# Gateloop attention with mixture of depths: 128-token tiles in place of 32-token chunks

## The chip, the cores and the metric

One core of a Trainium2 chip. The metric is device time in microseconds, the median of three runs. The engines in the traces: PE is TensorE (PEld its weight loads), DVE VectorE, ACT ScalarE, POOL GpSimd, SP SyncE, which issues the loads and stores.

## The reference

Four batches, 8 heads, 768 tokens, head size 48. Each head keeps a complex 48 x 48 state that decays and turns by a gate of each token and takes in k v; the output is q times the real part. The heads side by side give 384 columns, on which a mixture of depths works: of each batch's 768 tokens the 128 with the largest score pass a two-layer network and are added back, times a sigmoid of their score.

```python
mag = np.sqrt(a_re * a_re + a_im * a_im)
scale = np.minimum(mag, 0.999) / (mag + 1e-06)
a_re_n, a_im_n = (a_re * scale, a_im * scale)
for t in range(S):
    ar, ai = (a_re_n[:, :, t, :, None], a_im_n[:, :, t, :, None])
    new_re = ar * S_re - ai * S_im
    new_im = ar * S_im + ai * S_re
    kv = np.einsum('bhd,bhe->bhde', k[:, :, t], v[:, :, t])
    S_re, S_im = (new_re + kv, new_im)
    y[:, :, t] = np.einsum('bhd,bhde->bhe', q[:, :, t], S_re)
...
for b in range(B):
    top_idx = np.argpartition(-scores[b], capacity)[:capacity]
    xe = x[b, top_idx]
    ye = np.maximum(xe @ w1, 0.0) @ w2
    g = 1.0 / (1.0 + np.exp(-scores[b, top_idx]))
    out[b, top_idx] = x[b, top_idx] + g[:, None] * ye
```

The inputs: a_re is uniform between 0.85 and 0.95, a_im normal with a spread of 0.1.

## The kernel before

The recurrence is turned into matmuls. The logs of the decays and the phases are summed along the tokens by triangular matrices on PE; their exponentials (E for the queries, Ei for the keys) and cosines and sines multiply q and k, so that a token pair's decayed score is a product of 96 numbers per head (48 cosine and 48 sine parts). A tile is 128 tokens; there are 24 tiles, six in a batch, and everything is float32.

- `gates(g)`, for a group of two tiles: logs and angles on ScalarE, GpSimd and DVE; `within` sums the log decays inside chunks of 32 tokens, relative to the chunk's middle (csl, L273); `across` gets the steps from middle to middle as 16 small matmuls (ms, L283) and a few DVE operations on m (L287 to L293); `phase` sums the turns of a tile (cst, L312) and adds the last row of the tile in front (L315), after which DVE takes the whole turns off (r and fg, L317 and L318); `absolute` and `sines` make cos and sin on ScalarE, for both tiles at once.
- `attention(g, c)`, for one tile: DVE turns q and GpSimd turns k (tq and tk, L352 and L355). `scores(hg)`, for four heads at a time: four PE transposes of q (L366) which ScalarE copies to SBUF (qT, L368), four of k (L371) which DVE copies in two halves of each chunk (kT, L376), then the scores of the first halves' keys against all queries (L383, 64 keys by 128 queries, PSUM partitions 0 to 63) and of the second halves' keys against the second halves' queries (L385, 64 by 64, PSUM partitions 64 to 127), and two predicated copies on DVE for the causal mask (L391). `inside` multiplies the masked scores with the values (L399), which for this are loaded a second time in another order (vh). Then for each of the four chunks `chunk(ci)`: DVE carries the state to the chunk's middle (G, L413), eight matmuls add its part to y (L415, 32 output rows), eight more form the chunk's own k v (d, L422, 32 tokens deep, 96 columns by 48), and DVE adds d to G (L428). `finish` copies y out and takes the score.
- `depths(b)`, for a batch: rank by comparing all scores, select 128 tokens, gather them (gx), two layers (hid, fin), scatter-add at the end.

The emitted order is woven: the gates run a group ahead of the scores, a tile's chunks run beside the next tile's scores, the depths a batch behind. A scheduler then sets each engine's queue, and the engines take their queues in order. PSUM has two buffers for csl, ms and cst together, two for the transposes (tp), and one each for the scores, d, y and the depths.

Of the kernel before, what the change touches and what calls it, by code (L numbers as in the profile page):

```python
# [14 lines left out]
OP = mybir.AluOpType  # L15
PSUM = bass.MemoryType.PSUM
# [5 lines left out]
CH = 32  # L22
HALF = CH // 2
NCH = P // CH
# Largest -log of a step's decay, exp(HALF * LNMAX) times a score still being a float32. A step that
# decays more counts as exp(-LNMAX).
LNMAX = 4.8
# [21 lines left out]
def kernel(  # L49
# [18 lines left out]
    DD = 2 * D  # L68
# [4 lines left out]
    C = 2  # L73
    W = C * DM
    GPB = NT // C
    NG = B * GPB
    NB = (capacity + P - 1) // P
    HG = 4

    singles = ctx.enter_context(tc.tile_pool(name="singles", bufs=1))  # L80
    ld = ctx.enter_context(tc.tile_pool(name="ld", bufs=2))
    tmp = ctx.enter_context(tc.tile_pool(name="tmp", bufs=1))
    grp = ctx.enter_context(tc.tile_pool(name="grp", bufs=2))
    pe_ = ctx.enter_context(tc.tile_pool(name="pe_", bufs=2))
    qkp = ctx.enter_context(tc.tile_pool(name="qkp", bufs=2))
    stp = ctx.enter_context(tc.tile_pool(name="stp", bufs=2))
    xp = ctx.enter_context(tc.tile_pool(name="xp", bufs=2))
    mod = ctx.enter_context(tc.tile_pool(name="mod", bufs=1))
    fp = ctx.enter_context(tc.tile_pool(name="fp", bufs=B if NB == 1 else 2))
    dr = ctx.enter_context(tc.tile_pool(name="dr", bufs=2, space=DRAM))  # L90
# [10 lines left out]
    def act(**kw):  # L101
        """An activation that needs its table: these stay in the order in which they are emitted."""
# [5 lines left out]
    def table(name):  # L108
        ins = nc.scalar.preload_act_table_set(name)
# [5 lines left out]

    def load(nm, src, g):
        b, s = divmod(g, GPB)
        t = ld.tile([P, C, DM], FP, tag=nm, name=nm, bufs=3 if nm == "v" else 2)
        nc.sync.dma_start(out=t, in_=src[b, s * C * P:(s + 1) * C * P].rearrange("(c p) m -> p c m", p=P))
        T[nm, g] = t.rearrange("p c m -> p (c m)")  # L120

    def load_halves(g):
        # the values again, the first halves of the chunks in front of the second ones
        b, s = divmod(g, GPB)
        t = ld.tile([P, C, DM], FP, tag="vh", name="vh", bufs=3)
        for c in range(C):
            t0 = (s * C + c) * P
            rows = v[b, t0:t0 + P].rearrange("(n f i) m -> f n i m", f=2, i=HALF)
            for f in range(2):
                nc.sync.dma_start(out=t[f * P // 2:(f + 1) * P // 2, c],  # L130
                                  in_=rows[f])
        T["vh", g] = t.rearrange("p c m -> p (c m)")

    def load_a(g):
        if g < NG:
            load("ar", a_re, g)
            load("ai", a_im, g)

    def load_qkv(g):
        if g < NG:  # L140
            for nm, src in (("q", q), ("k", k), ("v", v)):
                load(nm, src, g)
            load_halves(g)

    load_a(0)
    load_qkv(0)
    load_a(1)

# [10 lines left out]
    def keep(t, pattern, base, mul):  # L159
        nc.gpsimd.affine_select(out=t, in_=t, compare_op=OP.is_ge, fill=0.0, base=base, pattern=pattern,  # L160
                                channel_multiplier=mul)

    # causal[s, t]: s and t in one chunk, s <= t
    causal = ones([P, NCH, CH], "causal")
    keep(causal, [[-CH, NCH], [0, CH]], 0, 1)
    keep(causal, [[CH, NCH], [1, CH]], 0, -1)
    # wmat[s, t]: the steps between the chunk's middle and t, with their sign
    wmat = ones([P, NCH, CH], "wmat")
    keep(wmat, [[-CH, NCH], [0, CH]], 0, 1)
    keep(wmat, [[CH, NCH], [0, CH]], HALF - 1, -1)  # L170
    nc.vector.tensor_tensor(out=wmat, in0=causal, in1=wmat, op=OP.subtract)
    wmat = wmat.rearrange("p a b -> p (a b)")
    # between[s, c]: the steps from the middle of chunk c - 1 to that of chunk c; of the first chunk
    # those in this tile, and in the last column those from the last middle to the end
    between = ones([P, NCH + 1], "between")
    keep(between, [[-CH, NCH + 1]], HALF, 1)
    keep(between, [[CH, NCH + 1]], HALF - 1, -1)
# [5 lines left out]
    keep(last, [[0, P]], -(P - 1), 1)  # L183
    # earlier[i, j]: j < i
# [443 lines left out]
```

## Time and profile before

| what | value |
|---|---|
| runs | 878.3, 883.08, 887.25 us |
| median | 883.08 us |
| span of the profiled execution | 883.5 us |
| PE busy in it | 805.7 us |
| DVE busy in it | 410.5 us |
| ACT and POOL busy in it | 206.3 and 165.0 us |
| mean granted clock of TensorE | 0.629 |

The profiled execution has no time of its own beside its span; the span runs from the first to the last instruction and agrees with the median within 0.4 us. Busy times of engines overlap, so they don't add up. [...]

### The profile page before, as it was taken

To read this page: it belongs to the slowest core of one execution; us is meant where nothing else is said; L and a number is where in the kernel's file an instruction comes from. 1 tells how busy PE (TensorE), PEld (TensorE's weight loads), DVE (VectorE), ACT (ScalarE), POOL (GpSimd) and SP (SyncE) were. 2 spreads that over 40 slices of the span, in tenths; PEclk is the share of its full clock that TensorE was granted. 3 is DMA by queue.
4 is the path that set the end of the run, shared out by engine and by line. 5 is a ranking of instruction groups with operands and counts; after the bars stand their busy time and mean duration, and the time that the engine had idled before them with its cause. 6 is when DMAs were issued, how large, how long until landed. Compare 5 with 4: busy or idle time off the path is not lost. (4 is left out here: it accounts for less than half of the span.)

```text
span 883.5 us, 12759 instructions
## 1 busy us (share of the span) xinstructions
PE 805.7 (91%) x5452; PEld 669.5 (76%) x5452; DVE 410.5 (46%) x886; ACT 206.3 (23%) x296; POOL 165.0 (19%) x117
## 2 busy tenths in 40 slices
PE   1499999999999899999999989999999979999926
PEld 0388887887787688787887878889779759888824
DVE  5444734544426765424335654632533674543250
ACT  4241420321313213112221420511321311200000
POOL 6140500511302302111300400410220220100020
PEclk9975555555556587655557556855655756795559
DMA  8511201201203102011201301110210000000030
GB/s 234 185 55 46 81 1 54 72 2 58 69 1 92 52 19 64 19 27 46 72 10 45 99 1 36 56 35 1 67 60 1 28 10 1 10 10 1 10 54 10
DMA packets 25881, 39.57 MB, mean 45 GB/s; under 512 B 1736, under 2 KB 24928, under 8 KB 25824
## 3 DMA queue, kind: packets, MB, share of 16 engines
q1 hardware_dynamic: 25248, 37.96, 14.0%
q0 software_dynamic: 576, 0.79, 0.8%
q8 instruction: 43, 0.70, 0.4%
q14 instruction: 14, 0.11, 0.0%
HBM read 33.23 MB, written 5.52 MB: 44 GB/s over the span
## 5 line engine op out<-in xcount | busy, mean ns | idle before, releaser
L422 PEld LDWEIGHTS d<-v,tk 32*96 32x96 f32 x1472 | 217.7, 242 | 44.5 <-issue 14.6
L422 PE MATMUL d<-v,tk 32*96 32x48 f32 x1472 | 239.9, 330 | 11.1 <-POOL tk L355 6.2
L355 POOL TENSOR_TENSOR tk<-cos,ek 128x768 f32<-128x768 f32 x24 | 51.6, 2149 | 553.4 <-ACT cos L103 304.3
L415 PEld LDWEIGHTS y<-G,qT 96*32 96x32 f32 x1472 | 106.2, 153 | 27.7 <-issue 12.0
L415 PE MATMUL y<-G,qT 96*32 96x48 f32 x1472 | 121.9, 263 | 1.9 <-DVE G L413 1.9
L383 PE MATMUL at<-qT,kT 96*64 96x128 f32 x384 | 94.2, 396 | 0.0
L399 PEld LDWEIGHTS y<-vh,att 128*128 128x128 f32 x384 | 71.5, 272 | 11.8 <-issue 6.2
L368 ACT COPY qT<-tq 96x512 f32<-96x512 f32 x48 | 27.9, 582 | 219.5 <-PE tq L366 219.1
L399 PE MATMUL y<-vh,att 128*128 128x48 f32 x384 | 74.3, 351 | 2.4 <-DVE att L391 1.6
L391 DVE COPY_PREDICATED att<-ordered,at 128x256 f32<-128x256 uint32 x96 | 37.8, 426 | 79.6 <-PE at L385 79.3
L383 PEld LDWEIGHTS at<-qT,kT 96*64 96x64 f32 x384 | 62.0, 198 | 11.8 <-issue 3.6
L273 PE MATMUL csl<-ln,wmat 128*128 128x384 f32 x48 | 36.2, 884 | 30.1 <-DVE ln L265 30.1
L283 PEld LDWEIGHTS ms<-between,ln 128*96 128x96 f32 x384 | 56.5, 254 | 3.6 <-issue 3.3
L283 PE MATMUL ms<-between,ln 128*96 128x5 f32 x384 | 57.0, 285 | 0.9 <-issue 0.9
L371 PE MATMUL tk<-ident,tk 128*96 128x128 f32 x192 | 52.7, 399 | 1.3 <-ACT qT L368 1.3
L366 PE MATMUL tq<-ident,tq 128*96 128x128 f32 x192 | 53.9, 407 | 0.0
L385 PE MATMUL at<-qT,kT 96*64 96x64 f32 x384 | 53.7, 303 | 0.0
L376 DVE COPY kT<-tk 96x256 f32<-96x256 f32 x96 | 37.9, 413 | 29.9 <-PE tk L371 29.8
L385 PEld LDWEIGHTS at<-qT,kT 96*64 96x64 f32 x384 | 42.4, 198 | 10.8 <-issue 6.3
L437 ACT COPY x<-y 128x384 f32<-128x384 f32 x24 | 11.5, 479 | 146.8 <-PE y L415 146.5
L103 ACT ACTIVATE t<-t 128x768 f32<-128x768 f32 x48 | 40.5, 844 | 15.2 <-POOL t L250 13.7
L273 PEld LDWEIGHTS csl<-ln,wmat 128*128 128x128 f32 x48 | 13.4, 325 | 35.6 <-DVE ln L265 31.2
(283 smaller groups left out, 906.8 us busy)
## 6 DMA issues: line engine op xcount, KB each, us to landing
ar<-in_a_re_dram SPq DMA_DIRECT2D x12, 384.0 KB
ai<-in_a_im_dram SPq DMA_DIRECT2D x12, 384.0 KB
q<-in_q_dram SPq DMA_DIRECT2D x12, 384.0 KB
k<-in_k_dram SPq DMA_DIRECT2D x12, 384.0 KB
v<-in_v_dram SPq DMA_DIRECT2D x12, 384.0 KB
vh<-in_v_dram SPq DMA_DIRECT2D x48, 96.0 KB
out_dram<-x SPq DMA_DIRECT2D x24, 192.0 KB
w1s<-in_moe_w_dram SPq DMA_DIRECT2D x1, 1536.0 KB
```

The costliest lines, as they stand in the source:

```text
L103: ins = nc.scalar.activation(**kw)
L273: nc.tensor.matmul(out=cs.rearrange("p (h d) -> p h d", d=D), lhsT=wmat, rhs=T["ln", g][:, c * H:(c + 1) * H, 0, :], start=True, stop=True)
L283: nc.tensor.matmul(out=ms[0:DD, x], lhsT=T["ln", g][:, x].rearrange("p u d -> p (u d)"), rhs=between, start=(x == 0), stop=(x == C * H - 1 ...
L355: eng.tensor_tensor(out=t, in0=T["cos", g][:, hs], in1=xb, op=OP.mult)
L366: nc.tensor.transpose(out=tq[0:DD, j], in_=st["q"][:, hg * HG + j].rearrange("p u d -> p (u d)"), identity=ident)
L371: nc.tensor.transpose(out=tk[0:DD, j], in_=st["k"][:, hg * HG + j].rearrange("p u d -> p (u d)"), identity=ident)
L376: nc.vector.tensor_copy(out=kT[0:DD, f], in_=tk4[0:DD, :, :, f * HALF:(f + 1) * HALF])
L383: nc.tensor.matmul(out=at[0:P // 2, j], lhsT=k0, rhs=q4, start=(j == 0), stop=(j == HG - 1), skip_group_check=True)
L385: nc.tensor.matmul(out=at[P // 2:P, j, :, HALF:CH], lhsT=k1, rhs=q4[:, :, HALF:CH], start=(j == 0), stop=(j == HG - 1), skip_group_check=True)
L399: nc.tensor.matmul(out=y[:, h * D:(h + 1) * D], lhsT=st["at", hg][:, j], rhs=V(h, "vh"), start=(h == 0), stop=False, skip_group_check=True)
L415: nc.tensor.matmul(out=st["y"][rows, h * D:(h + 1) * D], lhsT=st["qT"][0:DD, h, rows], rhs=G[0:DD, h], start=False, stop=(ci == NCH - 1 an ...
L422: nc.tensor.matmul(out=d[0:DD, h], lhsT=st["k"][rows, h].rearrange("p u d -> p (u d)"), rhs=V(h)[rows], start=(h == 0), stop=(h == H - 1), ...
```

## The change

- Tiles instead of chunks. The log decays are summed from an origin that is set anew every three tiles (RT), two origins a batch: csl adds, beside its own triangle ("upto"), the full sums of the tiles in front by the matrix "every". E and Ei carry a shift of 31 in the exponent. `across` with its middles goes.
- The state d stays in one PSUM buffer and is summed there over the three tiles of an origin; each tile copies it, or adds the base of the first three tiles; at a new origin it is scaled by mcol, one column of E that 16 one-column matmuls (ms) bring to the partitions.
- Halves of 64 columns. The 48 cosine and 48 sine parts of a head stand at columns 0 and 64 (FO); scores, inside y, carried y, d and ms are each issued as two matmuls, for PSUM partitions from 0 and from 64. The mask of the scores is a multiplication by "upto". kT is copied in one piece of 512 columns for four heads, and vh is not loaded any more.
- The groups of the gates are one tile, two tiles, and then three tiles each; loads of q, k and v go by tile; both activation tables are loaded only where they change.
- At the end a flag is worked out: the largest summed decay (top) and whether all scores are numbers. All engines read it, and a second, exact path (`steps`, one token at a time) runs if it fails.

```diff
+RT = 3
+SHIFT = 31.0
+CMAX = 75.0
+FO = 64
...
+    sizes = [1, 2]
+    while sum(sizes) < N:
+        sizes.append(min(3, N - sum(sizes)))
...
-            load_halves(g)
...
+        def within(n):
             def f():
+                i = n % RT
+                before = T["ln", n - 1] if i > 0 else None
+                if i > 1:
+                    before = tmp.tile([P, DM], FP, tag="lsum", name="lsum")
+                    nc.gpsimd.tensor_tensor(out=before, in0=T["ln", n - 1],
+                                            in1=T["ln", n - 2] if i == 2 else T["lsum"], op=OP.add)
+                    T["lsum"] = before
                 cs = ps_c.tile([P, DM], FP, tag="cs", padded_shape=[P, 512], name="csl")
+                nc.tensor.matmul(out=cs, lhsT=upto, rhs=T["ln", n], start=True, stop=(i == 0))
+                if i > 0:
+                    nc.tensor.matmul(out=cs, lhsT=every, rhs=before, start=False, stop=True)
+                e, ei = (pe_.tile([P, DM], FP, tag=nm, name=nm) for nm in ("E", "Ei"))
+                act(out=e, in_=cs, func=AF.Exp, scale=-1.0, bias=up)
+                act(out=ei, in_=cs, func=AF.Exp, bias=down)
+                T["E", n], T["Ei", n] = e, ei
+                if i == RT - 1 or (n + 1) % NT == 0:
+                    nc.gpsimd.tensor_tensor(out=top[96:P], in0=top[96:P], in1=ei[96:P], op=OP.add)
+                if i == RT - 1 and (n + 1) % NT != 0:
+                    ms = ps_c.tile([P, H], FP, tag="cs", padded_shape=[P, 512], name="ms")
+                    for h in range(H):
+                        for o in (0, FO):
+                            nc.tensor.matmul(out=ms[o:o + D, h:h + 1], lhsT=e[:, h * D:(h + 1) * D],
+                                             rhs=ident[:, P - 1:P], start=(h == 0), stop=(h == H - 1),
+                                             skip_group_check=True)
...
         def scores(hg):
             def f():
+                at = ps_a.tile([P, HG, P], FP, tag="at", name="at")
                 for j in range(HG):
+                    for o in (0, P // 2):
+                        nc.tensor.matmul(out=at[o:o + P // 2, j], lhsT=st["k", hg][0:FR, j, o:o + P // 2],
+                                         rhs=st["q", hg][0:FR, j], start=(j == 0), stop=(j == HG - 1),
+                                         skip_group_check=True)
+                a = qkp.tile([P, HG, P], FP, tag="at", name="att", bufs=3)
+                nc.vector.tensor_tensor(out=a, in0=at, op=OP.mult,
+                                        in1=upto.rearrange("p (u t) -> p u t", u=1).to_broadcast([P, HG, P]))
...
+        def state():
+            if s == NT - 1:
+                return
             for h in range(H):
+                for u in range(2):
+                    nc.tensor.matmul(out=d[u * FO:u * FO + D, h], lhsT=st["k"][:, h, u * FO:u * FO + D], rhs=V(h),
+                                     start=(s % RT == 0 and h == 0), stop=(s % RT == RT - 1 and h == H - 1),
+                                     skip_group_check=True)
+            fresh = s % RT == RT - 1
...
+        def inside(hg):
...
+                for h in range(hg * HG, (hg + 1) * HG):
+                    for o in (0, P // 2):
+                        nc.tensor.matmul(out=st["y"][o:o + P // 2, h * D:(h + 1) * D],
+                                         lhsT=st["at", hg][:, h - hg * HG, o:o + P // 2], rhs=V(h),
+                                         start=(h == 0), stop=(s == 0 and h == H - 1), skip_group_check=True)
...
+        def carried(hg):
...
+                        nc.tensor.matmul(out=st["y"][o:o + P // 2, h * D:(h + 1) * D],
+                                         lhsT=st["q", hg][0:FR, h - hg * HG, o:o + P // 2],
+                                         rhs=T["S", n - 1][0:FR, h], start=False, stop=(h == H - 1),
+                                         skip_group_check=True)
...
+    fl = ps_m.tile([P, 1], FP, tag="m", padded_shape=[P, 512], name="fl")
+    nc.tensor.matmul(out=fl[0:1], lhsT=flag[:, 0:1], rhs=every[:, 0:1], start=True, stop=True)
+    ok = singles.tile([P, 1], I32, name="ok")
+    nc.vector.tensor_copy(out=ok[0:1], in_=fl[0:1])
+    rv = nc.values_load(ok[0:1, 0:1], min_val=0, max_val=P)
+    with tc.If(rv < P):
+        steps()
```

Where the instructions stand on PE before, in the middle of a batch: carried y and d of chunk after chunk, each y with its own state G, between the transposes of the next tile.

```order
L399 MATMUL y_2303<-vh_1373,att3_167 128x48 x4
L415 MATMUL y_2303<-G_2323,qT_2164 32x48 x8
L422 MATMUL d_2333<-v_1371,tk_2076 96x48 x8
L366 MATMUL tq_2399<-ident_124,tq_2318 96x128 x4
L371 MATMUL tk_2405<-ident_124,tk_2349 96x128 x3
L422 MATMUL d_2361<-v_1371,tk_2076 96x48 x5
L415 MATMUL y_2303<-G_2351,qT_2164 32x48 x8
L422 MATMUL d_2361<-v_1371,tk_2076 96x48 x3
```

And now, at a like place: inside y and carried y of a tile in halves, one state S for all of the tile, and d of the next tile in the one buffer d_161.

```order
L390 MATMUL d_161<-v_514,tk0_157 48x48 x5
L365 MATMUL tq_1008<-ident_122,tq1_155 112x128 x4
L415 MATMUL y_1015<-v_514,att_951 64x48 x8
L365 MATMUL tk_1024<-ident_122,tk1_159 112x128 x4
L415 MATMUL y_1015<-v_514,att_972 64x48 x8
L365 MATMUL tq_1045<-ident_122,tq1_155 112x128 x4
L426 MATMUL y_1015<-S__828,qT_843 64x48 x8
L426 MATMUL y_1015<-S__828,qT_881 64x48 x5
L365 MATMUL tk_1060<-ident_122,tk1_159 112x128 x4
```

The four chunks with their G are gone; a tile's y is 16 halves of inside and 16 of carried, and between them stand only transposes.

PE before, at the end of a group's gates: the last cst (fg_2548 goes on to the cosines of the next group), and what follows it.

```order
L315 MATMUL cst_2600<-fg_2548,last_147 128x384
L385 MATMUL at_2621<-qT_2606,kT_2618 64x4x16
L383 MATMUL at_2621<-qT_2606,kT_2618 64x128
L385 MATMUL at_2621<-qT_2606,kT_2618 64x4x16
L415 MATMUL y_2486<-G_2633,qT_2398 32x48 x8
L422 MATMUL d_2643<-v_1756,tk_2349 96x48 x2
L371 MATMUL tk_2663<-ident_124,tk_2551 96x128 x2
L399 MATMUL y_2705<-vh_1758,att2_165 128x48 x4
L422 MATMUL d_2735<-v_1756,tk_2551 96x48 x5
```

And now, at the end of the gates of the third group: cst_628 is the last one, and tk1_159 and tq1_155 behind it are turned by the new cosines.

```order
L320 MATMUL cst_607<-fr_569,last_139 128x384
L318 MATMUL cst_628<-ai_239,turns_134 128x384
L426 MATMUL y_711<-S__534,qT_553 64x48 x3
L426 MATMUL y_711<-S__534,qT_597 64x48 x8
L320 MATMUL cst_628<-fr_569,last_139 128x384
L390 MATMUL d_161<-v_377,tk1_159 48x48
L365 MATMUL tq_704<-ident_122,tq1_155 112x128 x4
L365 MATMUL tk_723<-ident_122,tk1_159 112x128 x4
```

Before, 18 rows of the old tile stood between the last cst and the first transposes of the next group (tq_2801); now d and tq follow the last cst directly here, and behind two or three rows of halves at later groups.

## Rows read from the trace of the kernel before

**Rows 1.** The page, parts 1 and 2: busy time, granted clock in tenths.

```profile
PE 805.7 (91%) x5452; PEld 669.5 (76%) x5452; DVE 410.5 (46%) x886; ACT 206.3 (23%) x296; POOL 165.0 (19%) x117
...
PEclk9975555555556587655557556855655756795559
```

**Rows 2.** Busy time by stage: stretch, its length, each engine, clock, DMA.

```profile
0.00:44.00 44.00, 13.88 (x48) 9.11 (x49) 21.14 (x35) 16.58 (x21) 18.75 (x35) 0.96 0.71 210
44.00:836.00 792.00, 770.44 (x5272) 642.82 (x5271) 375.59 (x799) 187.33 (x270) 139.93 (x79) 0.61 0.12 37
836.00:883.50 47.50, 21.42 (x138) 17.54 (x136) 13.78 (x53) 2.36 (x5) 6.32 (x4) 0.72 0.18 30
```

**Rows 3.** Span and mean granted clock of the core.

```profile
core 0: 883.5 us, clock 0.629
```

**Rows 4.** Waits: who for whom, us in total, times, longest.

```profile
ACT qT L368 <- PE tq L366: 219.1, 42, 14.9
...
PE csl L273 <- DVE ln L265: 30.1, 6, 17.9
```

**Rows 5.** Chain of waits, in order of time: start, us, what.

```profile
664.25 5.05 PE ms L283 x32
669.30 2.72 PE d L422 x16
...
674.40 1.42 PE y L415 x16
676.20 0.85 PE tk L371 x4
...
773.44 4.71 PE fin L550 x14
```

**Rows 6.** Timeline of PE over old scores: start, us, instruction.

```profile
313.48 0.42 PE L385 MATMUL at<-qT,kT 96*64 96x64 f32 x2
313.60 0.42 PE L383 MATMUL at<-qT,kT 96*64 96x128 f32 x1
313.70 0.42 PE L385 MATMUL at<-qT,kT 96*64 96x64 f32 x2
313.81 0.42 PE L383 MATMUL at<-qT,kT 96*64 96x128 f32 x1
313.91 0.42 PE L385 MATMUL at<-qT,kT 96*64 96x64 f32 x2
314.02 0.42 PE L383 MATMUL at<-qT,kT 96*64 96x128 f32 x1
```

**Rows 7.** Busy time by stage again, two stretches of 22 us.

```profile
110.00:132.00 22.00, 22.00 (x144) 19.35 (x144) 7.04 (x16) 5.00 (x8) 1.75 (x2) 0.50 0.01 1
770.00:792.00 22.00, 22.00 (x219) 17.76 (x217) 8.98 (x20) 2.25 (x4) 1.29 (x2) 1.00 0.02 5
```

**Rows 8.** Busy time by stage, sums of L413 and of L428 alone.

```profile
sum 883.50, DVE 64.55; mean DVE 21.52
...
sum 883.50, DVE 48.35; mean DVE 16.12
```

**Rows 9.** Groups of DVE instructions by line: busy us, mean ns, idle before.

```profile
L376 DVE COPY kT<-tk 96x256 f32<-96x256 f32 x96 | 37.9, 413 | 29.9 <-PE tk L371 29.8
L391 DVE COPY_PREDICATED att<-ordered,at 128x256 f32<-128x256 uint32 x96 | 37.8, 426 | 79.6 <-PE at L385 79.3
...
L265 DVE TENSOR_SCALAR ln<-t 128x1536 f32<-128x1536 f32 x12 | 22.6, 1884 | 24.1 <-POOL t L261 24.1
```

**Rows 10.** Timeline of the first group's end: start, us, instruction.

```profile
36.66 0.56 DVE L317 TENSOR_SCALAR r<-cst 128x384 f32<-128x384 f32 x1 [1.80 <-PE cst L315]
...
40.25 2.51 POOL L355 TENSOR_TENSOR tk<-cos,ek 128x768 f32<-128x768 f32 x1 [17.56 <-ACT cos L103]
...
42.82 0.39 PE L422 MATMUL d<-v,tk 32*96 32x48 f32 x1 [6.20 <-POOL tk L355]
```

More of the change, by code (lines that the diff above doesn't have):

```diff
@@ L157, in ones @@
         return t
[L159 to L177, printed above, removed]
+    upto = singles.tile([P, P], FP, name="upto")
+    make_upper_triangular(nc, upto, val=1.0, diag=True)
+    every = ones([P, P], "every")
     turns = singles.tile([P, P], FP, name="turns")
@@ L227, in gates, with part @@
     def gates(g):
-        def twice(t):
-            return t.rearrange("p (x u d) -> p x u d", u=1, d=D).to_broadcast([P, C * H, 2, D])
+        ns = groups[g]
+        C = len(ns)
+        W = C * DM
         ar, ai = T["ar", g], T["ai", g]
-        first = g % GPB == 0
-        t0, t1, t2, t3 = (tmp.tile([P, W], FP, tag="t%d" % i, name="t%d" % i) for i in range(4))
+        t0, t1, t2 = (tmp.tile([P, CM * DM], FP, tag="t%d" % i, name="t%d" % i)[:, 0:W] for i in range(3))
+        t3 = grp.tile([P, CM * DM], FP, tag="ln", name="t3")[:, 0:W]
+        def part(t, i):
+            return t[:, i * DM:(i + 1) * DM]
         def squares():
@@ L251, in angle, with decay @@
             act(out=t1, in_=t1, func=AF.Ln)
+        def decay():
+            nc.vector.scalar_tensor_tensor(out=t2, in0=t0, scalar=-0.5, in1=t2, op0=OP.mult, op1=OP.add)
+            nc.vector.tensor_scalar(out=t0, in0=t0, scalar1=0.5, scalar2=math.log(0.999), op0=OP.mult, op1=OP.min)
+            ln = (grp.tile([P, CM * DM], FP, tag="ln", name="ln") if g > 0
+                  else grp.tile([P, W], FP, tag="ln0", name="ln0", bufs=1))
+            nc.gpsimd.tensor_tensor(out=ln[:, 0:W], in0=t2, in1=t0, op=OP.subtract)
+            for i, n in enumerate(ns):
+                T["ln", n] = part(ln, i)
         def angle2():
@@ L316, in f @@
[L316 to L324 removed]
+                    nc.tensor.matmul(out=cs, lhsT=last, rhs=T["fr", n - 1], start=False, stop=True)
@@ L331, in sines @@
[L331 to L339 removed]
+            cos = T["cosg", g][:, 0:C * H]
+            fr3 = T["frg"].rearrange("p (x d) -> p x d", d=D)
+            nc.vector.tensor_scalar(out=cos[:, :, 0].bitcast(I32), in0=fr3.bitcast(I32), scalar1=0x7FFFFFFF,
+                                    scalar2=None, op0=OP.bitwise_and)
@@ L440, in finish @@
-            nc.vector.scalar_tensor_tensor(out=junk, in0=x, scalar=1.0, in1=wgb, op0=OP.mult, op1=OP.mult,
-                                           accum_out=T["sc", b][:, s:s + 1])
-        return ([turned("q", nc.vector), turned("k", nc.gpsimd)] + [scores(hg) for hg in range(H // HG)],
-                [inside] + [chunk(ci) for ci in range(NCH)] + [finish])
+            score(b, s)
+        G = range(H // HG)
+        return ([turned("q", nc.vector), turned("k", nc.gpsimd)],
+                [across(nm, hg) for hg in G for nm in "qk"] + [scores(hg) for hg in G],
+                [state] + [f(hg) for f in (inside, carried) for hg in G] + [finish])
@@ L573 @@
+    load_qkv(1)
+    load_w()
     for f in gates(0):
         f()
-    state = []
-    for i in range(NG):
-        load_qkv(i + 1)
-        load_a(i + 2)
-        if i == 0:
-            load_w()
-        recur = []
-        for c in range(C):
-            score, follow = attention(i, c)
-            weave(*((0.0, 1.0, [lambda f=f: recur.append(f) for f in fs]) for fs in (score, state)))
-            state = follow
-        ahead = gates(i + 1) if i + 1 < NG else []
-        behind = depths((i - 1) // GPB - 1) if i > 1 and i % GPB == 1 else []
-        weave((0.0, 0.95, ahead), (0.0, 1.0, recur), (0.05, 1.0, behind))
@@ L589 @@
-    for f in state:
-        f()
+    done, queue, behind = 0, [], []
+    follow = []
+    for n in range(N + 1):
+        load_qkv(n + 2)
+        if n < N:
+            g, i = where[n]
+            if i == 0:
+                load_a(g + 2)
+                queue = gates(g + 1) if g + 1 < len(groups) else []
+                share = -(-len(queue) // len(groups[g]))
+            ahead, queue = queue[:share], queue[share:]
+            prep, score_, after = attention(n)
+        else:
+            ahead, prep, score_, after = [], [], [], []
+        b, s = divmod(n - 1, NT)
+        if n > NT and s == 0:
+            behind = depths(b - 1)
+            slice_ = -(-len(behind) // (NT - 1))
+        some, behind = behind[:slice_ if behind else 0], behind[slice_ if behind else 0:]
+        weave((0.0, 0.2, prep), (0.1, 1.0, score_), (0.0, 0.95, ahead), (0.0, 0.9, follow), (0.05, 1.0, some))
+        follow = after
```

397 lines of the change are left out of this document (210 added, 187 removed).

## Prediction

> **What bounds the kernel now.** I read the page's first two parts, then busy time by stage, then the list of waits, and last the chain of waits for the price of one record of each kind. TensorE is busy 805.7 of 883.5 us, and the PEclk line shows a clock near half for most of the run [rows 1]. By stage [rows 2] the stretch from 44 to 836 us holds nearly all of it: 770.4 us of PE in 792 at a clock of 0.61, beside 375.6 us of DVE. The mean clock is 0.629 [rows 3]. What waits there waits for PE: ScalarE's copies of the transposed queries alone sat 219.1 us behind the transposes, while the worst wait of PE's own comes to 30.1 us [rows 4]. So the time is PE's stream at the granted clock, plus idle PE: 883.5 - 805.7 = 77.8 us, of which 44.0 - 13.9 = 30.1 lie at the start, 21.6 in the long middle and 47.5 - 21.4 = 26.1 in the last stretch. The profiled span lies 0.4 us above the median of the runs shown (883.08), so a sum made against the one stands for the other.
>
> **The price of the stream.** Every fp32 matmul is two records. [...] I use 0.212 for every record whose weights or moving side are 128 wide, and 0.672 for every 384-wide one. Before, with both records: 68 csl and cst matmuls 91; 964 that are 128 wide (192 each of tq, tk, the L383 scores, inside y; 72 gx, 24 ex, 96 hid, 4 scT) 409; fin 43; ms 61; carried y 131; d 250: 985 us. The L385 scores cost nothing, for they run beside L383 (below). At clock 0.629 this is 985 x 0.5/0.629 = 783; the trace has 805.7, so I carry a factor 1.029 for switches and run ends.
>
> **What the change makes of it.** The 736 d matmuls of 32 tokens, whose 96 weight columns cost more than their 48 moving ones, become 320 of 128 tokens and 48 columns; the 736 carried y become 320, the 192 inside y become 384 halves, the scores 384 halves, and 64 one-column matmuls replace the 192 ms. Sixteen 384-wide matmuls with "every" are added; transposes stay at 384. All halves come as pairs that write PSUM partitions 0 and 64. What a pair costs is shown by the old scores [rows 6]: between 313.48 and 313.91 four L385 records start, one per 0.107 us, while L383 records start every 0.21, as if either were alone. So I take a pair as one: a score record 0.212, a y record (64 weight columns, as L385) 0.107. For d and ms (48 columns) I take 0.089, the carried y's row. Sum at the lower level: 84 wide ones 113; 772 of 128 (384 transposes, 192 pairs of scores, 196 in the depths) 327; fin 43; y 352 pairs 75; d 28; ms 6: 592, with the factor 610 us against 1014 before. The other bound has halves one after another: 81 + 75 + 28 + 6 = 190 more, 783, with the factor 806.
>
> [...] The trace disagrees at this place: 64-column weights are loaded for both streams of rows 6 and neither is slowed.
>
> **The clock.** It is the largest unknown. Between 770 and 792 us the clock stood at 1.00 and 219 records went through without a gap; between 110 and 132 us it stood at 0.50 with 144 [rows 7]. The first is a mix of fin, transposes, scores and chunks, the second mostly chunks, ms and d, in which the array waits for weights half the time. d and ms fall from 311 of 985 us to 34 of 592, so the new stream is mostly streams that move on every cycle; that speaks for the upper level. Against it: PE will stand and wait more often (below), and the middle as a whole stood at 0.61 though PE hardly waited there. Between 0.5 and 0.95 I take 0.8: PE 610 x 0.5/0.8 = 381 us; at 0.95 it is 321, at 0.629 485, at 0.5 610.
>
> **The other engines.** DVE loses G (64.6) and S (48.4) [rows 8], the doubled ln (22.6) [rows 9] and the small operations on m, and gains 20 state updates of 48.4/88 = 0.55: 11. Forty-eight copies of 512 columns replace 96 of 256; at an estimated 0.68 us, between 0.55 for 384 columns and twice 0.413, that is 33 instead of 38, and the masking of the scores is alike, 33 for 38 [rows 9]. So DVE goes from 410.5 to about 275 us, 11 a tile; ScalarE and GpSimd hardly move from 206.3 and 165.0 [rows 1]. Nothing of these is over PE's 381/24 = 16 us a tile, but DVE is no longer far below: at the upper level PE has 13.
>
> **Idle PE, term by term.** Start: 30.1 us now. The first group shrinks to one tile, but the second and third have two and three, and only 16 us of PE a tile to lie beside; I take 40 (25 to 60). Group boundary: the first tile of a group needs its cosines, and the only such stretch that stands bare in the trace runs from DVE's r at 36.66 to the first d at 42.82, 6.2 us for two tiles [rows 10]; with three the absolute value and two Sin grow by half, so 7.3. In the old order some eighteen rows stand between the last cst and the next tile's transposes; in the new one none at the third group, and 20 to 35 halves (1 to 4 us) at later ones. I take 3.5 us at seven boundaries: 25 (0 to 51). Within a tile: PE now comes back to DVE for two kT, two masked scores and one state, with single PSUM buffers for scores, y and state; each trip is an operation of about 0.7 us plus whatever stands ahead of it in DVE's queue, against 0.6 to 0.9 us of other matmuls. I take 0.7 us uncovered each, 3.5 a tile over 21 tiles: 74 (22, what the middle loses now, to 130). Behind the waiting PE stand the next tile's transposes, and behind those ScalarE's and DVE's copies. Tail: the last depths are unchanged, 26; reading the flag on five engines and the jump over the stepwise path are not in the trace, 0 to 12, I take 5. Without the vh loads the queue of SP is only lighter: DMA is busy 0.12 of the middle stretch [rows 2]. Idle is 40 + 25 + 74 + 31 = 170.
>
> Sum: 381 + 170 = 551, say **550 us**. Low end 339 (clock 0.9) + 25 + 26 + 10 + 60 = 460; high end 485 (clock as now) + 60 + 38 + 40 + 67 = 690.
>
> **Rivals.** A, the clock stays at 1.2 GHz: PE 610 us, waits mostly covered since PE is slow: 610 + 40 + 31 + 10 + 22 = 713. For it: the run sat there most of the time although PE was 91% busy, and transposes rise from 163 of 985 us to 163 of 592. Against it: stretch 770 to 792, transposes among it, at 1.00. [...]
> B, the clock stays up and the scheduler hides the trips: 321 + 25 + 31 + 20 + 60 = about 457. For it: the middle loses only 21.6 us now. Against it: that was with PE at twice DVE's time.
> C, slower: the halves don't run beside one another, so the change doesn't do what it says, and the half-filled array never earns the upper level. Its place is each pair of scores, y, d and ms; its price is 190 us of stream: 806 + 40 + 31 + 10 + 22 = 909. It decides only below a clock of about 0.52; at 0.629 it gives 641 + 103 = 744, still faster. Rows 6 speak against it.
> The exact path, 3072 steps of more than 20 small DVE operations, would be many milliseconds. It runs if 384 steps sum to over 75 of -log decay; with a_re of at least 0.85 they reach 384 x 0.163 = 62, so it doesn't.
>
> **How the numbers follow.** Forecast 0.65, A 0.15, B 0.16, C 0.04. The range 460 to 690 holds the forecast with its bounds and half of B; outside lie A, C and the other half of B, near 2 in 10 after A's and B's nearer edges. A measurement of this kernel tells about 1% from no change: forecast, A, B and a part of C are faster (0.96), 0.01 within 1%, 0.03 slower.
>
> **What would show it.** In the new profile: PE busy 370 to 400 us at a mean clock near 0.8; two score records of a pair starting together; DVE 265 to 285 us; PE's largest waits on DVE's att and kT and on GpSimd's tk at the groups' first tiles; a tail of about 45 us. Wrong would be a clock under 0.65 (A), PE waits under 40 us in the middle (B), or starts of a pair's records that alternate (C).

## The result and the profile after

The changed kernel takes 480.6 us (median of four runs, 477.1 to 481.2) against 883.6 in the same session: a ratio of 0.543, 95% interval 0.540 to 0.546. Forecast were 550 us in a range of 460 to 690. The direction held, and so did the stream and the clock of the sum; the idle time did not. The time lies nearer to rival B's 457 than to the forecast.

The page after, parts 1 and 2, answers to [rows 1]:

```profile
PE 354.2 (74%) x3950; PEld 270.9 (57%) x3950; DVE 329.5 (69%) x576; ACT 188.0 (39%) x245; POOL 191.6 (40%) x115
...
PEclk9996678878988796959996997879977979995587
```

Span and mean granted clock of the core [rows 3], then busy time by stage [rows 2], in the same columns:

```profile
core 0: 478.6 us, clock 0.849
```

```profile
0.00:40.00 40.00, 15.66 (x100) 9.98 (x100) 20.71 (x42) 20.20 (x28) 22.60 (x30) 0.96 0.59 202
40.00:80.00 40.00, 26.98 (x286) 18.27 (x286) 28.81 (x33) 22.30 (x28) 24.48 (x13) 0.74 0.21 65
80.00:430.00 350.00, 289.64 (x3453) 224.12 (x3453) 266.56 (x446) 143.20 (x185) 138.16 (x69) 0.87 0.21 64
430.00:478.60 48.60, 21.93 (x115) 18.52 (x115) 13.43 (x57) 2.33 (x5) 6.32 (x4) 0.70 0.18 30
```

Read them as a sum. PE's busy time at the granted clock, brought to the lower level, is 354.2 x 0.849/0.5 = 601 us (605 when the four stages are worked out one by one), where it was 805.7 x 0.629/0.5 = 1014. The stream is 413 us shorter at the lower level, a clock of 0.50, and it ran at 0.849 instead of 0.629. Idle PE rose from 77.8 to 478.6 - 354.2 = 124.4 us: 37.4 in the first 80 us, 60.4 in the middle, 26.7 at the end. So span = 300.5/clock + idle, and this form is used below for every run.

What PE waited for (who for whom, us in total, times, longest):

```profile
PE d L390 <- POOL tk L356: 29.5, 7, 6.4
PE csl L279 <- POOL ln L261: 21.3, 7, 6.2
PE gx L521 <- DVE sel L512: 18.8, 3, 15.3
PE csl L279 <- DMA v<-in_v_dram: 10.0, 1, 10.0
PE at L376 <- DVE att L380: 9.5, 7, 2.9
...
PE tk L365 <- DVE kT L367: 3.4, 3, 1.3
```

The two largest are both on GpSimd, seven times each: 50.8 us. The one behind tk stands at the first tile of a group, the one behind ln where the next group's gates begin. Of the 50.8 us 36.4 lie between 80 and 430 us, 18.9 behind tk and 17.5 behind ln. The trips to VectorE (att, kT) are 13 us. The wait of 10.0 us put down to a load of v is the kernel's first csl, at 10.01 us, and its weight load waited as long for ln; in the runs below where ln is compared, this same wait of 10.0 to 12.4 us stands in the row of ln, so it is taken out of that row there.

One group boundary in the timeline of all engines (start, us, instruction):

```profile
88.69 0.91 PE L320 MATMUL cst<-fr,last 128*128 128x384 f32 x2
...
90.38 0.56 DVE L323 TENSOR_TENSOR fr<-cst,r 128x384 f32<-128x384 f32 x1
90.97 1.16 ACT L113 ACTIVATE cos<-fr 128x1152 f32<-128x1152 f32 x1 [1.70 <-DVE fr L323]
...
92.04 1.24 ACT L113 ACTIVATE cos<-cos,hpi 128x1152 f32<-128x1152 f32 x1
...
93.36 5.07 POOL L356 TENSOR_TENSOR tk<-cos,k 128x768 f32<-128x768 f32 x2 [13.93 <-ACT cos L113]
...
95.99 0.40 PE L390 MATMUL d<-v,tk 128*48 128x48 f32 x2 [6.39 <-POOL tk L356]
96.32 1.10 PE L365 MATMUL tq<-ident,tq 128*112 128x128 f32 x4
...
243.87 0.65 PE L365 MATMUL tq<-ident,tq 128*112 128x128 f32 x4
```

Up to 95.99 this is the chain the prediction named (DVE, two Sin, GpSimd's tk, then d), 6.4 us of it bare. What follows it costs something too. Busy time by stage of the wait, of the 4 us behind it, and of an undisturbed 4 us later on:

```profile
90.00:96.00 6.00, 0.01 (x1) 0.01 (x1) 4.35 (x5) 4.76 (x4) 2.64 (x2) 0.61 0.33 122
96.00:100.00 4.00, 4.00 (x21) 3.47 (x22) 1.77 (x3) 2.51 (x3) 2.43 (x1) 0.50 0.58 169
240.00:244.00 4.00, 4.00 (x27) 2.36 (x26) 4.00 (x3) 3.92 (x4) 3.65 (x2) 1.00 0.49 148
```

TensorE stood, the clock fell during the wait (1.00 from 90 to 91 us, 0.50 from 92 to 96), and the stream behind it ran at 0.50. Four tq records took 1.10 us there and take 0.65 at 243.87, where the clock is 1.00. Four us at 0.50 are, as an estimate from these two levels, 2 us more than the same work takes at 1.00.

It is not the only such place. Of the six other waits of over 3 us behind tk or ln after 80 us, these are three, each with the 4 us that follow it:

```profile
185.50:189.50 4.00, 2.12 (x23) 1.96 (x24) 4.00 (x7) 0.56 (x1) 2.04 (x1) 0.50 0.22 58
208.00:212.00 4.00, 4.00 (x22) 2.78 (x23) 2.85 (x3) 2.54 (x4) 2.04 (x2) 0.50 0.02 4
...
354.80:358.80 4.00, 4.00 (x21) 2.59 (x22) 3.97 (x8) 1.05 (x3) 3.93 (x3) 0.50 0.01 2
```

Behind the other three, from 112.3, 138.8 and 255.9, the clock is 0.64, 0.57 and 0.50. A wait of 5.0 us near the start, which ends at 23.8, is followed by 4 us at 1.00, so not every wait is paid for in this way.

### The profile page after: what moved, and what is told of

Its sections match the earlier page's. It is cut to its first block, busy times and chain, and to the rows that moved or that the text cites. A ratio compares the mean times of both kernels' runs of the same rounds, so it can differ in the third digit from the quotient of the medians.

```text
span 478.6 us, 9347 instructions
## 1 busy us (share of the span) xinstructions
PE 354.2 (74%) x3950; PEld 270.9 (57%) x3950; DVE 329.5 (69%) x576; ACT 188.0 (39%) x245; POOL 191.6 (40%) x115
## 4 chain that ended last, share of the span: by engine, by line
PE 42%; POOL 18%; DVE 18%; issue 13%; ACT 6%; DMA 2%; POOLq 0%; SPq 0%; ACTq 0%; DVEq 0%
PE hid L553 5%; POOL ln L261 5%; PE at L376 5%; POOL tk L356 5%; PE csl L279 4%; PE tq L365 4%; PE gx L521 4%; PE y L415 3%; PE tk L365 3%; POOL ai L267 3%; PE y L426 3%; PE d L390 2%; ACT t L113 2%; POOL t L252 2%; PE fin L561 2%
## 5 line engine op out<-in xcount | busy, mean ns | idle before, releaser
L356 POOL TENSOR_TENSOR tk<-cos,k 128x768 f32<-128x768 f32 x24 | 54.6, 2287 | 146.4 <-ACT cos L113 133.2
L376 PE MATMUL at<-qT,kT 112*64 112x128 f32 x768 | 58.9, 294 | 9.8 <-DVE att L380 9.5
L376 PEld LDWEIGHTS at<-qT,kT 112*64 112x64 f32 x768 | 46.1, 147 | 22.8 <-issue 11.5
L367 DVE COPY kT<-tk 112x512 f32<-112x512 f32 x48 | 32.9, 686 | 33.0 <-PE tk L365 32.9
L279 PE MATMUL csl<-ln,upto 128*128 128x384 f32 x48 | 31.0, 748 | 31.4 <-POOL ln L261 21.3
L390 PE MATMUL d<-v,tk 128*48 128x48 f32 x640 | 27.4, 227 | 29.5 <-POOL tk L356 29.5
L113 ACT ACTIVATE t<-t 128x1152 f32<-128x1152 f32 (+2 forms) x36 | 38.1, 1057 | 22.5 <-POOL t L252 21.0
L356 DVE TENSOR_TENSOR tq<-cos,q 128x768 f32<-128x768 f32 x24 | 40.7, 1707 | 7.8 <-ACT cos L113 7.0
L365 PE MATMUL tq<-ident,tq 128*112 128x128 f32 x192 | 38.7, 330 | 3.9 <-ACT qT L367 2.0
L365 PE MATMUL tk<-ident,tk 128*112 128x128 f32 x192 | 36.2, 317 | 6.3 <-DVE kT L367 3.4
L380 DVE TENSOR_TENSOR att<-at,upto 128x512 f32<-128x512 f32 x48 | 32.9, 685 | 11.6 <-PE at L376 11.4
L353 POOL TENSOR_TENSOR k<-k,Ei 128x384 f32<-128x384 f32 x24 | 29.5, 1230 | 26.7 <-ACT Ei L113 26.1
L415 PEld LDWEIGHTS y<-v,att 128*64 128x64 f32 x768 | 31.1, 151 | 12.7 <-issue 10.3
L415 PE MATMUL y<-v,att 128*64 128x48 f32 x768 | 36.3, 238 | 0.7 <-DVE att L380 0.7
L365 PEld LDWEIGHTS tk<-ident,tk 128*112 128x112 f32 x192 | 26.1, 156 | 10.3 <-DVE kT L367 4.2
L252 POOL TENSOR_TENSOR t<-t,t 128x1152 f32<-128x1152 f32 (+2 forms) x9 | 24.8, 2754 | 15.5 <-ACT t L113 15.5
```

The costliest lines, as they stand in the source:

```text
L113: ins = nc.scalar.activation(**kw)
L252: nc.gpsimd.tensor_tensor(out=t1, in0=t3, in1=t1, op=OP.add)
L279: nc.tensor.matmul(out=cs, lhsT=upto, rhs=T["ln", n], start=True, stop=(i == 0))
L353: eng.tensor_tensor(out=x, in0=x, in1=T[e, n], op=OP.mult)
L356: eng.tensor_tensor(out=t[:, :, :, 0:D], in0=T["cos", n], in1=xb, op=OP.mult)
L365: nc.tensor.transpose(out=ps[0:FR, j], in_=st[nm][:, hg * HG + j, 0:FR], identity=ident)
```

## Experiments

Twelve more kernels ran, on three chips, each beside the kernel before; the ratio is what compares them. "Stream" is PE busy x clock/0.5, the stream at the lower level; "idle" is span less PE busy. Span, clock and both columns come from the profiled execution, the median from the timed runs, the ratio is to the kernel before on the same chip.

| run | median us | ratio (95%) | clock | stream | idle |
|---|---|---|---|---|---|
| changed kernel | 480.6 | 0.543 (0.540-0.546) | 0.849 | 601 | 124.4 |
| halves joined | 507.6 | 0.573 (0.570-0.576) | 0.831 | 658 | 110.9 |
| no flag | 479.6 | 0.542 (0.537-0.546) | 0.856 | 599 | 126.1 |
| mask twice | 473.3 | 0.534 (0.530-0.538) | 0.892 | 605 | 128.2 |
| gates early | 460.9 | 0.520 (0.517-0.523) | 0.880 | 600 | 118.2 |
| before, wide d and y | 743.0 | 0.841 (single runs 0.820 to 0.857) | 0.700 | 891 | 101.8 |
| before, full array | 631.4 | 0.713 (0.710-0.716) | 0.844 | 873 | 113.6 |
| gates in two tiles | 466.3 | 0.529 (0.525-0.533) | 0.891 | 603 | 122.5 |
| gates on VectorE | 444.8 | 0.505 (0.501-0.508) | 0.898 | 595 | 109.7 |
| origin per tile | 505.8 | 0.574 (0.569-0.578) | 0.824 | 612 | 131.3 |
| ln wait filled | 476.3 | 0.538 (0.535-0.541) | 0.888 | 644 | 113.6 |
| VectorE and early | 437.1 | 0.494 (0.492-0.496) | 0.908 | 592 | 109.5 |
| VectorE and two tiles | 438.8 | 0.495 (0.492-0.499) | 0.886 | 599 | 102.6 |

**Halves joined.** Scores, both y and d as one matmul per head:

```diff
-for o in (0, P // 2):
-    nc.tensor.matmul(out=at[o:o + P // 2, j], lhsT=st["k", hg][0:FR, j, o:o + P // 2], ...)
+nc.tensor.matmul(out=at[:, j], lhsT=st["k", hg][0:FR, j], ...)
```

> Every pair of 64-column halves becomes one matmul: scores 128 weight columns, both y products 128, d 112. If a pair costs what one half costs alone, the stream grows at the lower clock level by 704 y records x (0.212 - 0.107) = 74 us and 320 d records x about (0.198 - 0.089) = 35 us, the scores stay: 592 + 109 = 701, with the factor 1.029 721 us. Theory 1, these 1344 records in which the array waits for weights also pull the clock down, to about 0.70: PE 515 us, time about 600 to 630. Theory 2, pairs are cheap but the clock stays at 0.85: PE 425 us, time 530 to 550. Rival, halves run one after the other, so that joining them saves or costs nothing: 470 to 485.

Measured: 507.6 us. Groups of PE instructions by line, after:

```profile
L376 PE MATMUL at<-qT,kT 112*64 112x128 f32 x768 | 58.9, 294 | 9.8 <-DVE att L380 9.5 <-ACT x L434 0.3
...
L415 PE MATMUL y<-v,att 128*64 128x48 f32 x768 | 36.3, 238 | 0.7 <-DVE att L380 0.7
...
L390 PE MATMUL d<-v,tk 128*48 128x48 f32 x640 | 27.4, 227 | 29.5 <-POOL tk L356 29.5
```

and with the halves joined:

```profile
L375 PE MATMUL at<-qT,kT 112*128 112x128 f32 x384 | 61.1, 308 | 10.9 <-DVE att L379 10.9
L412 PE MATMUL y<-v,att 128*128 128x48 f32 x384 | 56.0, 296 | 1.2 <-DVE att L379 1.2
L388 PE MATMUL d<-v,tk 128*112 128x48 f32 x320 | 43.1, 287 | 25.2 <-POOL tk L356 25.2
```

The 768 half records of the scores take no more time than the 384 whole ones (58.9 against 61.1 us): a pair costs what one costs. For d and the inside y, whose weight columns outnumber their 48 moving columns once joined, joining costs 15.7 and 19.7 us; the carried y goes from 28.6 to 48.1. Rival C (halves in series) falls. PE's busy time rose by 42 us and the time by 27, because idle PE fell by 13.5. The clock went from 0.849 only to 0.831 (four runs 0.828 to 0.832, against 0.845 to 0.862), not to 0.70: theory 1 falls as well. If the joined d and y records pulled the clock down, it was by no more than this 0.018. Time came out below theory 2's 530 since the stream grew by 57 us, not 109.

**No flag.** Everything from `flag = singles.tile(...)` to `steps()` is taken out.

> Left out: the range test at the end (its reduction, two matmul records, the read of the flag on five engines) and the stepwise path behind it. Theory, the flag lies beside the last scatter: 0 to 5 us less, 476 to 481. Rival, reading the flag on five engines and jumping over the path costs over 8 us after the scatter: 472 or less.

Measured: 479.6, an interval that holds the changed kernel's. The flag and the jump cost nothing that these runs can tell; their intervals leave room for about 5 us. In the changed kernel's own profile the last stretch loses 26.7 us of PE, as 26.1 before, so the 5 us of the prediction's tail do not show there.

**Mask twice.** The VectorE multiplication of `att` stands twice.

> VectorE masks each block of scores twice, 48 x 0.685 = 33 us more on it, and the single score buffer comes free that much later. Theory, TensorE's trips to VectorE are covered by other matmuls: 481 to 490. Rival, the trips stand bare as the prediction had them (74 us of them): the full 33 us, 505 to 515.

Measured: 473.3, below both ranges and not slower at all. VectorE did do the work (355.0 us busy against 329.5). Waits of PE in this run:

```profile
PE at L376 <- DVE att L382: 28.1, 15, 3.9
PE d L392 <- POOL tk L356: 21.6, 5, 6.6
...
PE csl L279 <- POOL ln L261: 18.2, 8, 10.0
```

The wait behind att grew from 9.5 to 28.1 us, so the trips are not all covered by other matmuls, as the theory had it. But the wait behind tk shrank by 7.9 us, and the one behind ln, without the first csl's 10.0, from 21.3 to 8.2, so idle PE is only 3.8 us more. That PE, coming later to a group's start, finds GpSimd's result readier is the likely reason; it is argued, not shown. The time went down by the clock: among this kernel's four runs the one at 0.859 took 479.5 us, those at 0.892 and 0.893 469.1 and 471.6. Why the clock stood higher is not settled. One difference is on record: in the middle stretch (from 80 us to 48.6 before the end) PE is idle for 63 us at a clock of 0.92, in the changed kernel for 60.4 at 0.87, but here only two of its waits last over 3 us, there seven.

**Gates early.** One number in the weaving of the lists:

```diff
-weave(..., (0.0, 0.95, ahead), ...)
+weave(..., (0.0, 0.6, ahead), ...)
```

> The next group's gate steps are spread over the first 0.6 of each tile's list and not over 0.95, so that the cosines of a group's first tile are asked for earlier. Theory, TensorE's 29.5 us behind GpSimd's first tk is a matter of order: that wait falls under 12 us, time 455 to 470. Rival, it is the gate chain's own work (GpSimd, ScalarE and VectorE in turn), and the wait only moves: 475 to 486.

Measured: 460.9, inside the theory's range, but the named wait fell only to 25.3 us from 29.5, not under 12. The row of ln reads 28.4 us, 17.6 without the first csl's 10.8, against 21.3. Idle fell by 6 us, the clock rose to 0.880, worth 13 us of PE. The order matters; that it matters through tk's wait alone is not shown.

**Gates in two tiles.** The list of a group's gate steps is divided by two and not by three:

```diff
-share = -(-len(queue) // len(groups[g]))
+share = -(-len(queue) // min(2, len(groups[g])))
```

> The next group's gate steps all stand in the first two tiles of a group of three, none in the third, so the cosines come a tile earlier. Theory, the order sets TensorE's waits behind GpSimd's first tk (29.5 us) and its clock after them: that wait under 8 us, time 440 to 465. Rival, bunched gate steps delay VectorE's kT and att of these two tiles by as much: 470 to 490.

Measured: 466.3, a little outside both ranges, with tk's wait at 24.4 us. Listing the steps earlier did not bring the cosines a tile forward: in this run's timeline GpSimd's tk still follow on the last Sin directly. What holds the chain in front of them back was not separated.

```profile
178.42 1.25 ACT L113 ACTIVATE cos<-cos,hpi 128x1152 f32<-128x1152 f32 x1
...
179.74 4.66 POOL L356 TENSOR_TENSOR tk<-cos,k 128x768 f32<-128x768 f32 x2 [16.10 <-ACT cos L113]
...
181.96 0.56 PE L390 MATMUL d<-v,tk 128*48 128x48 f32 x6 [5.01 <-POOL tk L356]
```

**Gates on VectorE.** Three operations per group change engine:

```diff
-nc.gpsimd.tensor_tensor(out=ln[:, 0:W], in0=t2, in1=t0, op=OP.subtract)
+nc.vector.tensor_tensor(out=ln[:, 0:W], in0=t2, in1=t0, op=OP.subtract)
```

> The three long gate operations on GpSimd (22.2 + 21.2 + 21.2 us) go to VectorE, 21 operations of an estimated 1.2 to 1.8 us. Theory, GpSimd's length sets TensorE's 21.3 us behind ln, and its operations slow VectorE's (tq 1.71 us now, 1.03 before): ln wait under 10, tq under 1.3 us, time 460 to 470. Rival, VectorE is in order and already 69% busy, the 25 to 38 us more come back as waits behind kT and att: 480 to 500.

Measured: 444.8, 7% below the changed kernel and below the theory's own range. Its waits and groups:

```profile
PE d L390 <- POOL tk L356: 21.3, 4, 6.5
...
PE csl L279 <- DVE ln L261: 14.6, 6, 10.3
```

```profile
10.26 1.62 PE L279 MATMUL csl<-ln,upto 128*128 128x384 f32 x2 [10.26 <-DVE ln L261]
```

The second line is the kernel's first csl: 10.3 of the 14.6 us are its wait.

```profile
L356 DVE TENSOR_TENSOR tq<-cos,q 128x768 f32<-128x768 f32 x24 | 35.5, 1491 | 10.0 <-ACT cos L113 7.0 <-PE tq L365 3.0
...
L367 DVE COPY kT<-tk 112x512 f32<-112x512 f32 x48 | 32.6, 684 | 29.5 <-PE tk L365 29.5
...
L353 DVE TENSOR_TENSOR q<-q,E 128x384 f32<-128x384 f32 x24 | 15.7, 659 | 0.8 <-ACT E L113 0.7
...
L261 DVE TENSOR_TENSOR ln<-t,t 128x1152 f32<-128x1152 f32 x7 | 9.4, 1348 | 0.0
```

and the same operations in the changed kernel:

```profile
L356 DVE TENSOR_TENSOR tq<-cos,q 128x768 f32<-128x768 f32 x24 | 40.7, 1707 | 7.8 <-ACT cos L113 7.0 <-PE tq L365 0.8
L353 DVE TENSOR_TENSOR q<-q,E 128x384 f32<-128x384 f32 x24 | 22.7, 951 | 3.7 <-ACT E L113 3.7
...
L261 POOL TENSOR_TENSOR ln<-t,t 128x1152 f32<-128x1152 f32 x7 | 22.2, 3169 | 4.4 <-DVE t L258 4.4
```

The ln operation of 1152 columns takes 1.35 us here and 3.17 on GpSimd in the changed kernel. GpSimd's busy time fell by 69 us, VectorE's did not rise (327.6 against 329.5), since others of its operations got faster. Idle fell by 15 us and PE's busy time by 23, about 19 of it by the clock (300.5/0.849 - 300.5/0.898). So these three operations, where they stood on GpSimd, held the changed kernel back by 7%. The run changes two things at once, a shorter chain of gates and a faster VectorE, and does not tell their shares. Of the two detailed expectations the one for ln was met (4.3 us behind it without the first csl, from 21.3); tq fell to 1.49 us and not under 1.3.

**Origin per tile.** `RT = 1`: the state is multiplied by the decay after every tile, no matmul carries the log sum across tiles.

> One decay origin per tile instead of one per three; the state is multiplied by the decay after every tile. Goes: 32 csl records with the matrix of ones (17.0 us), the sums of logs on GpSimd (8.4). Comes: ms for 20 tiles instead of 4 (640 records for 128, about 15 us more), 16 more products and scalings on VectorE (about 14 us), 16 more range sums on GpSimd (20 us). Theory, the longer origin is worth little by itself, the gain is in the 128-token tile: 478 to 495. Rival, the shorter chain to csl helps more than the rest costs: 460 to 475.

Measured: 505.8, above both ranges. The longer origin is worth 25 us, more than its operations: the stream grows by 11 us, idle by 7, and the clock falls to 0.824. The 31.2 us that PE waits behind ln here are no sign of it: without the first csl's 10.8 they are 20.4, against 21.3. Which of the added operations does it was not separated.

**The clock of the kernel before.** Two runs of the old kernel ask why it stood at 0.629. In the first, d and carried y of a chunk stream all 384 columns through head 0's weights:

```diff
-for h in range(H):
-    nc.tensor.matmul(out=d[0:DD, h], lhsT=st["k"][rows, h]..., rhs=V(h)[rows], ...)
+nc.tensor.matmul(out=d[0:DD], lhsT=st["k"][rows, 0]..., rhs=T["v", g][rows, c * DM:(c + 1) * DM]..., ...)
```

> The kernel before, with its d and its carried y of a chunk each as one matmul of 384 moving columns instead of eight of 48 (all heads take head 0's weights, so d and y are computed only in part). The stream at the lower level stays nearly what it was: 985 - 250 - 131 + 2 x 184 records x 0.672 = 851, with the factor 876. Theory, the clock of the kernel before was held at 1.2 GHz by runs in which the array waits for weights: the clock rises to 0.8 or more, PE to about 550, time 600 to 660. Rival, it was held there by something else (32 of 128 rows or columns in use, or PE being busy almost without a break): clock 0.60 to 0.68, time 720 to 800.

In the second the same matmuls also use the whole array (`rows` becomes all 128 tokens for d, and all 128 columns of qT for y):

> As the run with the wide d and y of the kernel before, but each d contracts all 128 tokens instead of 32 rows, and each carried y takes 128 weight columns instead of 32 (the values are not the reference's, d and y are computed only in a part and too often). Records and moving columns are the same, 876 us at the lower level. Theory, the clock of the kernel before was low because its matmuls fill a quarter of the array: clock 0.8 or more, time 560 to 660. Rival, the fill of the array doesn't matter to the clock: 0.66 to 0.73, time 715 to 760 as before this edit.

Both compute d and y only in part. Measured: 743.0 us (724 to 757) at clock 0.70 (four runs 0.67 to 0.71), and 631.4 at 0.844 (0.82 to 0.84). Cores and groups of the first, then of the second:

```profile
core 0: 738.4 us, clock 0.700
```

```profile
L420 PE MATMUL d<-v,tk 32*96 32x384 f32 x184 | 115.2, 716 | 16.0 <-POOL tk L355 8.6 <-DVE S__2842 L427 2.8 <-DVE S__1475 L427 2.3
L414 PE MATMUL y<-G,qT 96*32 96x384 f32 x184 | 97.8, 679 | 6.5 <-DVE G L413 6.3
```

```profile
core 0: 630.9 us, clock 0.844
```

```profile
L420 PE MATMUL d<-v,tk 128*96 128x384 f32 x184 | 93.8, 596 | 18.1 <-POOL tk L355 6.2 <-DVE S__2158 L427 1.6 <-DVE S__3155 L427 1.6
L414 PE MATMUL y<-G,qT 96*128 96x384 f32 x184 | 93.2, 599 | 8.1 <-DVE G L413 8.1
```

Records, moving columns and the stream at the lower level (891 and 873 us) are alike. What differs is how many rows or columns of the array they use (d 32 rows or 128, y 32 columns or 128), and with it the values they compute, which no run varied alone; the clock goes from 0.70 to 0.844. One matmul of 384 columns in place of eight of 48, on 32 rows or columns as before, brought 0.629 to 0.70. So the first run's theory falls (it asked for 0.8 and 600 to 660 us), and its rival's time range holds; in the second run the theory's clock and range hold. Of the 0.215 between 0.629 and 0.844 the wider d and y brought 0.07, the full array 0.144. The traces give the clock as a share of full and not in GHz; the level that the first run's theory names is their 0.50.

**ln wait filled.** Four matmuls that are overwritten stand before a group's first csl:

```diff
+if where[n][1] == 0 and g > 1:
+    for _ in range(4):
+        nc.tensor.matmul(out=cs, lhsT=every, rhs=w1s[:, 0, 0:DM], start=True, stop=True)
 nc.tensor.matmul(out=cs, lhsT=upto, rhs=T["ln", n], ...)
```

> Four more matmuls of 384 columns (weights of ones, moving columns from w1, overwritten by the next) stand in front of a group's first csl, where TensorE waited 21.3 us in all for GpSimd's ln: 7 x 8 records x 0.16 to 0.32 = 9 to 18 us more stream. Theory, each such wait lets the clock fall, and the price of a wait is the slower stream behind it: clock 0.88 or more, time 460 to 476 although there is more work. Rival, the wait costs its own length only: clock 0.85, time 481 to 495.

Measured: 476.3, at the edge of the theory's range, at a clock of 0.888. No run shows the 0.16 to 0.32 us a record of the expectation; the added 56 took 0.43 us each:

```profile
L281 PE MATMUL csl<-w1s,every 128*128 128x384 f32 x56 | 24.3, 572 | 0.0
```

24.3 us of added matmuls, and the kernel is not slower. At the old clock the stream of 644 would have taken 644 x 0.5/0.849 = 379 us; it took 362.8, and idle PE fell by another 10.8. The wait behind ln went from 21.3 to 12.4 us (24.8 on its row, 12.4 of it the first csl), the one behind tk from 29.5 to 17.5, and the middle stretch has four waits of over 3 us instead of seven. This agrees with the rows behind the waits above: a wait can cost more than its length, since a stretch at a clock of 0.50 to 0.64 followed each of those seven, and useless work in its place bought about its own cost back. It is no proof by itself, for the clock of the run with the mask twice rose as far (0.892 in the profiled execution) without any filling.

**Both remedies.** GpSimd's three operations on VectorE, with either change of order.

> GpSimd's three gate operations on VectorE, and the gate steps in the first 0.6 of each tile's list. Theory, the two remedies add, one shortens the chain and the other starts it earlier: 422 to 436. Rival, both remove the same waits, or VectorE (328 of 441 us) is now the limit of the middle: 440 to 450.

> GpSimd's three gate operations on VectorE, and all gate steps in the first two tiles of a group of three. Theory, the remedies add: 425 to 438. Rival, VectorE is then crowded in two tiles of three and its kT and att come late: 442 to 460.

Measured: 437.1 and 438.8, each just above its theory's range. Both are faster than VectorE alone, by 8 and 6 us where the order alone had brought 20 and 14, so they add in part only. That they remove partly the same waits is likely, not shown: in the first, idle PE is that of VectorE alone (109.5 against 109.7 us) and the gain is all in the clock and the stream. It has the lowest median of this study, 0.494 of the kernel before, but not clear of the second.

## Why the prediction was right and where it was off

**The stream** (610 us at the lower level): 601 measured. Its prices per record are those of [rows 5], at a clock of 0.50 from 664 to 678 us: a transpose 0.85/4 = 0.212 us, d 2.72/16 = 0.170, carried y 1.42/16 = 0.089, ms 5.05/32 = 0.158. The 0.672 for 384 columns is an estimate, twice fin's 4.71/14 = 0.336 at a clock of 1.00. The step on pairs, that two halves cost what one costs, is shown by the joined run; its parts were rougher than their sum, since d, y and the scores together grew by 57 us when joined and not by 109. That the sum comes within 2% is in part luck. It counts two records for every fp32 matmul, and a transpose is one: 24 tiles of 8 heads leave 192 records of tq, before and after.

```profile
L366 PE MATMUL tq<-ident,tq 128*96 128x128 f32 x192 | 53.9, 407 | 0.0
```

```profile
L365 PE MATMUL tq<-ident,tq 128*112 128x128 f32 x192 | 38.7, 330 | 3.9 <-ACT qT L367 2.0 <-DVE tq L356 1.9
```

So 388 records too many (192 tq, 192 tk, 4 scT) at 0.212, or 82 us, stand in both sums. The factor 1.029, taken from the old kernel, hid it: with 985 - 82 = 903 it would have been 1014/903 = 1.12, and the new stream (592 - 82) x 1.12 = 573, 28 us less than measured.

**The clock** (0.8, bounds 0.5 to 0.95): 0.849. Of the 72 us between the forecast's sum of 551 and the span of 478.6, 381 - 354 = 27 come from the stream and its clock. The direction was right, the reason only in part. The prediction held that d and ms, in which the array waits for weights, kept the clock down. Joined halves, whose weight columns outnumber the moving ones as well, brought it only to 0.831; in the old kernel 384 moving columns for d and y brought 0.70, and with all 128 rows for d and all 128 columns for y 0.844.

**Idle PE** (170 us): 124.4, the other 46. Start 40: 37.4 over the first 80 us. Group boundary 25: 29.5 behind tk, of the kind forecast, 18.9 of it after the first 80 us. But a second wait of this kind, 21.3 us behind GpSimd's ln (17.5 after the first 80), was not in the sum; the prediction said GpSimd would hardly move, and it went from 165.0 to 191.6 us. Tail 31: 26.7, with nothing for the flag.

**The trips within a tile** (74 us, 3.5 a tile): this is the step that failed. The trace has 13 us behind att and kT, and the whole middle has 60.4 us idle where the sum had 25 + 74 = 99. The step took every trip as bare by the operation's own 0.7 us. In the trace PE waited behind att before 7 of the 48 blocks of scores and behind kT 3 times; the other trips were covered by other matmuls. The cover is no deeper than that: with the mask twice it was 15 of 48 blocks and 28.1 us. Even so, those 25.5 us more of VectorE left the idle sum almost as it was. A trip in front of a group's start may use up waiting that PE would do there anyway, behind the gate chain; that the chain costs the kernel time is shown by the run with the gates on VectorE, the trade between the two waits is argued.

**VectorE** (about 275 us): 329.5. The parts taken from rows were right (kT 686 and att 685 ns for an estimated 680). The parts taken as unchanged were not: tq went from 1.03 to 1.71 us, q from 0.75 to 0.95 (last section), which makes 21 of the 54 us; the rest lies in many smaller operations. It cost little directly, since PE waited little for VectorE.

**The rivals.** C fell by the joined run, A, which had the clock stay at the level of 0.50, by the 0.849. That the share of transposes holds the clock down, as A's argument had it, no run shows: the records of tq and tk are 192 each before and after, at 0.629 and at 0.849. B came nearest: the trips were mostly hidden, but not at the clock of 0.95 it assumed, and the middle's 60.4 us of waiting are above the 40 that the prediction set as B's sign. Of the signs for the forecast, PE busy at 370 to 400 us, VectorE at 265 to 285 and large waits on att and kT did not come; the clock near 0.8, the waits on tk and the tail of about 45 us did.

## What to carry to other kernels

Write a sum for PE as stream/clock plus idle, and price a wait by its length and by the slower stretch that may follow it (here 4 us at 0.50 to 0.64 behind seven waits of over 3 us). In this kernel narrow matmuls cost twice, in records (736 d matmuls for 320) and in the clock (0.70 for d and y on 32 rows or columns, 0.844 on the full array). Two 64-column halves on the two halves of PSUM cost what one whole matmul does for the scores (58.9 us against 61.1) and less for d and inside y (27.4 against 43.1 us, 36.3 against 56.0), whose weight columns outnumber their moving ones when joined. When the engine that bounds a kernel gets twice as fast, look for the chain that runs beside it: here it was three long operations on GpSimd (3.17 us for one that VectorE does in 1.35), and moving them was worth more than any change of order.

## What the runs showed of the hardware that was not expected

In the kernel before with wide d and y, matmuls on 32 rows or 32 columns left the mean clock at 0.70, where as many records on the full array, with other values, ran at 0.844.

Several of VectorE's operations on inputs in SBUF took longer in the changed kernel than with GpSimd's three gate operations gone: q 951 ns against 659, tq 1707 against 1491, t (L257) 1831 against 1347, while the copies out of PSUM stayed at 686 and 684. It does not hold for all of them: ai (L306) went from 1351 to 1493. GpSimd's own k (L353) also went the other way, from 1230 to 1656 ns. What of GpSimd's work made the difference was not separated.
